# Making Q ahead of attention in seven Strassen products, and one pass of attention over K and V

## The chip, the cores and the metric

The kernel runs on one core of one Trainium2 chip. A core has five engines with instruction queues of their own: TensorE (PE, matmuls and transposes, its weight loads shown apart as PEld), VectorE (DVE), ScalarE (ACT), GpSimd (POOL) and SyncE (SP), from whose queue nearly all transfers are issued here. The time is the device time of an execution in microseconds, as the median of several runs. All arithmetic is float32. A product of two float32 matrices is made of three float32r matmuls: each operand is split into a high part (the value copied to float32r) and a low part (the difference), and high x low, low x high and high x high are added up in PSUM.

## The reference

One transformer block: layer norms modulated by a condition vector, attention against a cached K and V, and a gated FFN.

```python
def _A_ref(x, k_cache, v_cache, wq, wo):          # x (1, 2048, 576), caches (1, 16, 2048, 128)
    Hq, Dh = 32, 128
    W = min(4096, max(256, Sk // 4))              # 512: the last 512 keys
    q = (x @ wq).reshape(B, Sq, Hq, Dh).transpose(0, 2, 1, 3)
    k = jnp.repeat(k_cache[:, :, Sk - W:, :], 2, axis=1)      # 16 K/V heads, 32 query heads
    v = jnp.repeat(v_cache[:, :, Sk - W:, :], 2, axis=1)
    scores = jnp.einsum("bhqd,bhkd->bhqk", q, k) * (Dh ** -0.5)
    o = jnp.einsum("bhqk,bhkd->bhqd", _softmax(scores), v)
    return o.transpose(0, 2, 1, 3).reshape(B, Sq, Hq * Dh) @ wo

def _B_ref(x, w_gate, w_up, w_down):              # F = 4608
    return (_sigmoid(x @ w_gate) * (x @ w_up)) @ w_down

sa, ca, ga, sb, cb, gb = split(_silu(c) @ w_mod, 6)
h = _layernorm(x) * (1 + ca) + sa
x = x + ga * _A_ref(h, ...)
h = _layernorm(x) * (1 + cb) + sb
return x + gb * _B_ref(h, ...)
```

## The kernel before, in words

The 2048 tokens are four blocks of 512. The program has three stages: attention with the Q projection inside it, the output projection (`wo`), and the FFN. The last two are already made of seven Strassen products in place of eight block products; the operand sums that these need on the weight side are made during attention as background work, and parked in DRAM (`wosc`, `wsc`, `dsc`).

Attention runs over a list `seq` of 128 pairs of a head and a block: first all 32 heads for blocks 0 and 1 (half 0), then all 32 heads for blocks 2 and 3 (half 1). K and V of a group of two heads are therefore loaded and prepared twice (`load_k`, `make_k`, `load_v`, `make_v`, over `range(2 * HKV)`). Wq's columns of a head are also loaded and split once per half (`load_q`, `split_q`, `split_q_lo`).

A pair has four steps, one for each tile of 128 queries, and the main loop counts 512 of them. In step n TensorE is given a quarter of the Q projection of the pair two ahead (`qproj`, 14 matmuls a pair: four chunks of 128 channels with three each, and two for the last 64 channels, stacked twice into 128 rows), the three score matmuls of step n+2 (`scores`), four transposes of the probabilities of step n (`transp`), and three matmuls with V for the pair before (`pv`). VectorE takes each row's negative maximum from the scores (`neg`), ScalarE the exponential (`pp`) and the sum. After the transposes ScalarE copies them to float32r (the high part of `ptt`) and VectorE makes the low part. When a pair is through, the reciprocals of its sums go to DRAM (`put_rs`, tile `rscr`) and come back spread over the partitions (`get_rs`, tile `rb`), and VectorE multiplies the result of `pv` with them (`ov`); `put_o` writes it to DRAM (`oscr`).

Background work is laid out by a planner: each job gets one or two rooms (the tiles of x that are not in use), a start step, and further steps for its sums on GpSimd, its splits on ScalarE and GpSimd and its stores. There are 36 `ab` jobs (gate and up weights of 128 columns), 9 `tail` jobs (their last 32 rows) and 34 wide jobs (`wo` and `down`). A step's jobs are given out ahead of its attention work (`at_n`), or behind it (`at_late`). From step 8 on most instructions may be moved by the scheduler; those that pass `pin` or `keep_order` keep their program order, all DMAs among them.

All four blocks' normalised rows are turned into channel-major operands (`hT`), 20 transposes a block: block 0 at the start, block 1 in the first steps, blocks 2 and 3 in the middle, before half 1.

Of the kernel before, what the change touches and what calls it, by code (L numbers as in the profile page):

```python
# [9 lines left out]
F32 = mybir.dt.float32  # L10
# [6 lines left out]
P = 128  # L17
# [27 lines left out]
def adaln_block_kernel(ctx: ExitStack, tc: tile.TileContext, x, k_cache, v_cache, wq, wo, w_gate, w_up, w_down,  # L45
# [25 lines left out]
    wctx, actx = ExitStack(), ExitStack()  # L71
    wp = wctx.enter_context(tc.tile_pool(name="wp", bufs=1))
    ps = actx.enter_context(tc.tile_pool(name="ps", bufs=1, space=bass.MemoryType.PSUM))
    psw = actx.enter_context(tc.tile_pool(name="psw", bufs=1, space=bass.MemoryType.PSUM))

    def psum(tag, bufs, shape):
        return (psw if tag == "wo" else ps).tile(shape, F32, tag=tag, name=tag, bufs=bufs)

    def ps_sc():
        return psum("st", 4, [P, BLK])  # L80

    def ps_pt():
        return psum("st", 4, [P, BLK])

    def ps_qp():
        return psum("qp", 1, [P, BLK])

    def ps_ot():
        return psum("ot", 2, [P, BLK])

    def ps_wide():
        return psum("wo", 1, [P, BLK])

    def ps_wo():
        return ps_wide()[:, :D2]

    def raw_tile(shape):
        return wp.tile(shape, F32, tag="raw", name="raw", bufs=4)
# [3 lines left out]

    ident = const.tile([P, P], F32, name="ident")

# [10 lines left out]


# [8 lines left out]
    busy = raw_tile([P, P])  # L125
    nc.vector.memset(busy, 0.0)
    idle = ps_sc()
# [4 lines left out]
    tc.nc.gpsimd.memset(ones, 1.0)  # L132
    cexp = const.tile([P, NC + 1], F32, name="cexp")

# [7 lines left out]
    def mod_load(m):  # L142
        ws = []
        for j in range(2):
            w = wp.tile([P, NC, D2], F32, tag="wa", name="wm", bufs=4)
# [16 lines left out]
    def mod_half(row, j, add, loaded):  # L162
        p = ps_wo()
# [3 lines left out]

    xs = []

    for b in range(NB):  # L170
        xs.append(const.tile([P, TPB, D], F32, tag=f"x{b}", name=f"x{b}"))
# [5 lines left out]
    def bg_view(b, off, shape):  # L177
# [3 lines left out]
        v = xs[b].rearrange("p t d -> p (t d)")[:, off : off + n]  # L181
# [6 lines left out]
    LN = {}  # L188
# [41 lines left out]
    def load_a(w, n0):  # L230
        raw = raw_tile([P, NC + 1, P])
        keep_order(nc.sync.dma_start(raw[:, :NC, :], w[: NC * P, n0 : n0 + P].rearrange("(k p) n -> p k n", p=P)))
        for s in range(2):
            keep_order(nc.sync.dma_start(raw[s * TAIL : (s + 1) * TAIL, NC, :], w[NC * P :, n0 : n0 + P]))
        return raw

    def split_a_hi(raw):
        sp = wp.tile([P, 2 * NC + 1, P], F32R, tag="wa", name="wa", bufs=4)
        pin(nc.scalar.activation(sp[:, : NC + 1, :], raw, AF.Copy))
        return sp  # L240

    def split_a_lo(raw, sp):
        pin(nc.gpsimd.tensor_sub(sp[:, NC + 1 :, :], raw[:, :NC, :], f32(sp[:, :NC, :])))
        pin(nc.gpsimd.tensor_sub(sp[TAIL:, NC, :], raw[TAIL:, NC, :], f32(sp[TAIL:, NC, :])))

    def pairs_a(sp, hT):
        main, tail = hT
        out_ = []
        for k in range(NC):
            out_.append((sp[:, k, :], main[:, NC + k, :]))  # L250
            out_.append((sp[:, NC + 1 + k, :], main[:, k, :]))
            out_.append((sp[:, k, :], main[:, k, :]))
        out_.append((sp[:, NC, :], tail[:, 1, :]))
        out_.append((sp[:, NC, :], tail[:, 0, :]))
        return out_

    def load_b(w, n0):
        raw = raw_tile([P, D])
        keep_order(nc.sync.dma_start(raw, w[n0 : n0 + P, :]))
        return raw  # L260

    def split_b_hi(raw):
        sp = wp.tile([P, 2, D], F32R, tag="wb", name="wb", bufs=2)
        pin(nc.scalar.activation(sp[:, 0, :], raw, AF.Copy))
        return sp

    def split_b_lo(raw, sp):
        pin(nc.gpsimd.tensor_sub(sp[:, 1, :], raw, f32(sp[:, 0, :])))

# [8 lines left out]
    def down_mm(lhs_hi, lhs_lo, wb, j, p):  # L278
        cols = slice(j * D2, (j + 1) * D2)
        mm_seq(p, three(lhs_hi, lhs_lo, wb[:, 0, cols], wb[:, 1, cols]))  # L280
        return p


    hTs = {}
    at = actx.enter_context(tc.tile_pool(name="at", bufs=1, side="right"))

    def new_hT(b):
        main = wp.tile([P, 2 * NC, BLK], F32R, tag="hTm", name="hTm", bufs=2)
        tail = wp.tile([P, 2, BLK], F32R, tag="hTt", name="hTt", bufs=2)
        hTs[b] = (main, tail)  # L290

    sbc = at.tile([P, NC + 1, P], F32, tag="qt", name="sbc", bufs=2)
    extra = at.tile([P, 4 * P], F32, tag="rb", name="extra", bufs=2)
    scale, shift = mod_rows("scale"), mod_rows("shift")
    WM, EARLY, HN, NMR = {}, {}, {}, {}

    def load_mod(m, ks):
        if m not in WM:  # L300
            WM[m] = at.tile([P, NC + 1, D], F32, tag="ptt", name="wm0", bufs=2)
# [1292 lines left out]
```

## Time and profile before

| | |
|---|---|
| median of 3 runs | 3028.03 us (3025.97 to 3028.44) |
| the profiled execution | 3026.5 us from its first to its last instruction, which is its span |
| granted TensorE clock | 0.999 of full speed |
| first Q projection matmul | 22.89 us |
| first score row maximum, last one | 29.43 us, 1412.95 us |
| first matmul of the output projection | 1419.79 us |
| busy: PE, PEld, DVE, ACT, POOL | 3006.8, 2592.7, 2088.4, 1695.8, 1666.3 us |

Every instruction is recorded by one helper, so all have the line L36, and a group is told by its tiles: `qp<-hTm,wa` is the Q projection (`hTm`, `hTt` the channels, `wa` the split weights), `st<-kt,qt` scores, `st<-ident,pp` transposes of probabilities, `ot<-ptt,vs` the product with V, `qt<-qp` the split of Q; `x<-x` on GpSimd and ScalarE is background work, because x's tiles are its rooms. `sw<-sr,sw` is the low part of an FFN weight operand. A matmul's duration in the profile overlaps with that of the next, so the sum of durations is more than the time that passes; starts are to be compared. In a row of the grouped view stand the count, the busy time and the mean duration in ns, and the idle time of the engine before these instructions with what ended it.

### The profile page before, as it was taken

To read this page: it belongs to the slowest core of one execution; us is meant where nothing else is said; L and a number is where in the kernel's file an instruction comes from. 1 tells how busy PE (TensorE), PEld (TensorE's weight loads), DVE (VectorE), ACT (ScalarE), POOL (GpSimd) and SP (SyncE) were. 2 spreads that over 40 slices of the span, in tenths; PEclk is the share of its full clock that TensorE was granted. 3 is DMA by queue.
4 is the path that set the end of the run, shared out by engine and by line. 5 is a ranking of instruction groups with operands and counts; after the bars stand their busy time and mean duration, and the time that the engine had idled before them with its cause. 6 is when DMAs were issued, how large, how long until landed. Compare 5 with 4: busy or idle time off the path is not lost.

```text
span 3026.5 us, 49171 instructions
## 1 busy us (share of the span) xinstructions
PE 3006.8 (99%) x16644; PEld 2592.7 (86%) x16644; DVE 2088.4 (69%) x3685; ACT 1695.8 (56%) x3424; POOL 1666.3 (55%) x1558
## 2 busy tenths in 40 slices
PE   8999999999999999999999999999999999999999
PEld 7888888888888888888999988888888888888888
DVE  6666666677666666667888867666666876666667
ACT  5666666657666676555444654444444544444443
POOL 2334457634577887412555127766655566655565
PEclk9999999999999999999999999999999999999999
DMA  4677777776777777775547656555555565555554
GB/s 127 189 197 217 196 224 227 227 210 183 207 233 236 240 248 247 211 215 177 193 159 306 224 189 192 155 155 166 168 148 144 161 204 140 143 148 142 144 138 119
DMA packets 485788, 571.32 MB, mean 189 GB/s; under 512 B 52000, under 2 KB 434208, under 8 KB 476832
## 3 DMA queue, kind: packets, MB, share of 16 engines
q1 hardware_dynamic: 484400, 567.65, 63.1%
q8 instruction: 132, 2.16, 0.3%
q14 instruction: 120, 0.98, 0.1%
q10 hardware_dynamic: 1136, 0.53, 0.1%
HBM read 394.33 MB, written 173.70 MB: 188 GB/s over the span
## 4 chain that ended last, share of the span: by engine, by line
PE 94%; DVE 2%; issue 1%; POOL 1%; DMA 1%; ACT 1%; SPq 0%; POOLq 0%; DVEq 0%; ACTq 0%
PE a L36 21%; PE st L36 18%; PE w L36 13%; PE qp L36 13%; PE ot L36 11%; PE c L36 11%; PE b L36 5%; DVE x L36 1%; POOL x L36 1%; PE wo L36 1%; SPq L36 0%; DVE ptt L36 0%; ACT pp L36 0%; DVE neg L36 0%; DVE hc L36 0%
## 5 line engine op out<-in xcount | busy, mean ns | idle before, releaser
L36 DVE TENSOR_TENSOR x<-w,x 128x288 f32<-128x288 f32 x964 | 421.4, 452 | 249.4 <-PE w L36 246.8
L36 PE MATMUL a<-hc,sw 128*128 128x512 f32 x2016 | 583.4, 395 | 1.4 <-DVE v L36 1.3
L36 DVE TENSOR_REDUCE neg<-st 128x1 f32<-128x512 f32 x512 | 352.4, 688 | 275.6 <-PE st L36 274.9
L36 ACT ACTIVATE ptt<-st 128x512 fp32r<-128x512 f32 x512 | 306.0, 598 | 391.0 <-PE st L36 390.0
L36 PE MATMUL ot<-ptt,vs 128*128 128x512 f32 x1536 | 483.5, 423 | 1.8 <-DVE ptt L36 1.7
L36 PE MATMUL st<-kt,qt 128*128 128x512 f32 x1536 | 443.4, 395 | 0.4 <-ACT pp L36 0.4
L36 PE MATMUL qp<-hTm,wa 128*128 128x512 f32 x1524 | 440.5, 398 | 2.3 <-DVE hTm L36 1.2
L36 DVE TENSOR_TENSOR ptt<-st,ptt 128x512 fp32r<-128x512 f32 x512 | 351.9, 688 | 126.6 <-ACT ptt L36 126.3
L36 PEld LDWEIGHTS a<-hc,sw 128*128 128x128 f32 x2016 | 356.4, 188 | 41.6 <-DVE v L36 2.8
L36 ACT ACTIVATE pp<-st,neg 128x512 f32<-128x512 f32 x512 | 350.4, 684 | 43.7 <-DVE neg L36 42.6
L36 ACT ACTIVATE sw<-sr 128x384 fp32r<-128x384 f32 x504 | 257.9, 519 | 189.1 <-issue 90.0
L36 POOL TENSOR_TENSOR sw<-sr,sw 128x256 fp32r<-128x256 f32 x245 | 200.4, 819 | 282.8 <-ACT sw L36 282.6
L36 PEld LDWEIGHTS st<-kt,qt 128*128 128x128 f32 x1536 | 286.7, 188 | 66.9 <-ACT pp L36 1.1
L36 PEld LDWEIGHTS w<-wh,hl 128*128 128x128 f32 x1776 | 297.2, 188 | 51.2 <-DVE x L36 2.7
L36 PEld LDWEIGHTS qp<-hTm,wa 128*128 128x128 f32 x1524 | 281.5, 188 | 69.5 <-DVE qt L36 7.1
L36 PE MATMUL w<-wh,hl 128*128 128x288 f32 x1776 | 327.5, 296 | 0.4 <-DVE x L36 0.3
L36 POOL TENSOR_TENSOR x<-x 128x256 f32<-128x256 f32 (+3 forms) x342 | 254.4, 763 | 117.8 <-DMA x<-in_B_w_up_dram 58.6
L36 PEld LDWEIGHTS st<-ident,pp 128*128 128x128 f32 x2048 | 254.3, 140 | 70.4 <-ACT pp L36 0.8
L36 PE MATMUL st<-ident,pp 128*128 128x128 f32 x2048 | 307.0, 273 | 0.5 <-DVE ptt L36 0.3
L36 PE MATMUL c<-hc,sw 128*128 128x512 f32 x1008 | 302.9, 394 | 0.0
L36 DVE TENSOR_TENSOR sw<-sr,sw 128x256 fp32r<-128x256 f32 x259 | 189.9, 733 | 141.0 <-ACT sw L36 113.2
L36 PEld LDWEIGHTS ot<-ptt,vs 128*128 128x128 f32 x1536 | 252.9, 190 | 30.7 <-DVE ptt L36 4.2
(239 smaller groups left out, 5043.6 us busy)
## 6 DMA issues: line engine op xcount, KB each, us to landing
sr<-wsc SPq DMA_DIRECT2D x504, 192.0 KB
wh<-dsc SPq DMA_DIRECT2D x144, 288.0 KB
dsc<-x SPq DMA_DIRECT2D x34, 1008.0 KB
vr<-oscr SPq DMA_DIRECT2D x32, 1024.0 KB
rb<-rscr SPq DMA_DIRECT2D x126, 256.0 KB
wsc<-x SPq DMA_DIRECT2D x36, 896.0 KB
oscr<-ov SPq DMA_DIRECT2D x63, 512.0 KB
wosc<-x SPq DMA_DIRECT2D x32, 1008.0 KB
```

The source lines that it names most:

```text
L36: i = got(*args, **kw)
```

## The change

All of Q is made before attention begins. The 576 channels are two halves of 288, the 2048 tokens two pairs of blocks, and two heads that share K and V are taken together: a 2x2 block product, which takes seven products on sums of operands instead of eight. Each of the 32 units u (16 pairs of heads, for blocks 0 and 1 and then for blocks 2 and 3) has seven products of seven matmuls with 512 columns: twice three for 128 channels, and one for the last 32, whose three combinations are stacked into one operand of 128 rows. Weight sums are made by GpSimd (`w_sums`), weight operands split by ScalarE (high) and VectorE (low, two instructions: `w_split`). The channel sums T1 to T4 are made on the chip. Results are scaled, go to `qo` tiles, and are stored to DRAM (`qscr`) by SP. This takes 224 steps of one product each ahead of step 0. In the first 16 only block 0 is needed, and its products are kept in room tiles (`first_room`). Blocks 2 and 3 are normalised and turned in some 50 of the steps, 24 transposes a block.

Attention then runs over 16 groups with all four blocks of both heads in each, so K and V are loaded and prepared once. Q of a pair is loaded 13 steps ahead and split 6 steps ahead by ScalarE and GpSimd (`load_qt`, `split_qt`). In a step TensorE gets the scores of step n+2, the V product five steps behind, and the transposes, which have two PSUM banks of their own (`pt`). Background jobs are given out from step -200 on, in eight rooms instead of four, with other distances. All instructions up to the end of attention keep their program order.

On TensorE a step in the middle of attention was, with a piece of the Q projection on both sides:

```order
L36 MATMUL qp<-hTm,wa 128x512 x2
L36 MATMUL qp<-hTt,wa 128x512 x2
L36 MATMUL st<-kt,qt 128x512 x3
L36 MATMUL st<-ident,pp 128x128 x4
L36 MATMUL ot<-ptt,vs 128x512 x3
L36 MATMUL qp<-hTm,wa 128x512 x3
```

and now is, where K of the next group is transposed too:

```order
L36 MATMUL st<-kt,qt 128x512 x3
L36 MATMUL ot<-ptt,vs 128x512 x3
L36 MATMUL pt<-ident,pp 128x128 x4
L36 MATMUL st<-ident,kv 128x128 x4
L36 MATMUL st<-kt,qt 128x512 x3
```

The projection has left the step, and the V product stands ahead of the transposes.

On VectorE, in the first 16 products (`sw<-raw,sw` is the low part of a weight operand in two instructions, `qo<-b` a result's eviction, the others are block 1's channel operands and sums):

```order
L36 TENSOR_TENSOR x_111<-hs,x_111 128x512 x2
L36 TENSOR_TENSOR sw<-raw_77,sw 128x256
L36 TENSOR_TENSOR sw<-raw_77,sw 32x128
L36 SCALAR_TENSOR_TENSOR qc<-st,scol,qc 128x512 x2
L36 TENSOR_TENSOR qc<-x_111,qc 128x512 x2
L36 TENSOR_TENSOR x_111<-shift,x_111 128x512
L36 TENSOR_TENSOR sw<-raw_77,sw 128x256
L36 TENSOR_TENSOR sw<-raw_77,sw 32x128
L36 SCALAR_TENSOR_TENSOR qo<-b,x_114 128x512
```

These are new; the weight operands of the next products stand between them.

On SP, in the stretch of wide jobs, from before (`dsc`, `wosc` a wide job's stores, `in_B_w_down` its loads):

```order
L36 DMA rscr_284<-rs 128x4
L36 DMA x_101<-in_B_w_down_dram 128x288 x4
L36 DMA rb<-rscr_284 128x512
L36 DMA sscr_293<-sx 512x1x128
L36 DMA dsc_342<-x_104 128x2016
L36 DMA dsc_342<-x_103 128x2016
L36 DMA rscr_281<-rs 128x4
L36 DMA raw<-in_A_k_cache_dram 128x512
L36 DMA rb<-rscr_281 128x512
```

and of the change:

```order
L36 DMA rscr_335<-rs 128x4
L36 DMA qr<-qscr_3_134 128x512
L36 DMA rb<-rscr_335 128x512
L36 DMA wosc_408<-x_113 128x7x288
L36 DMA wosc_408<-x_112 128x7x288
L36 DMA xr_4663<-in_A_wo_dram 128x288 x4
L36 DMA rscr_336<-rs 128x4
L36 DMA qr<-qscr_3_134 128x512
L36 DMA rb<-rscr_336 128x512
```

Between the store of a pair's reciprocals and their load now stands the load of a Q.

The diff, cut to its core:

```diff
+    def load_raw(u):
+        raw, n0 = RAW[u % 2], u % HKV * 2 * P
+        t = raw.rearrange("p s (h n) d -> p s h (n d)", h=2)
+        for h in range(2):
+            nc.sync.dma_start(t[:, 0:2, h], wqh[: 2 * P, h, n0 : n0 + 2 * P].rearrange("(s p) n -> p s n", p=P))
+        for r in range(3):
+            nc.sync.dma_start(t[r * TQ : (r + 1) * TQ, 2], wqh[2 * P :, :, n0 : n0 + 2 * P])
...
+    def w_split(u, a, src=None):
...
+        t = SWQ[u, a] = sw_tile([P, 5, P])
+        nc.scalar.activation(t[:, 0:3, :], src, AF.Copy)
+        nc.vector.tensor_sub(t[:, 3:5, :], src[:, 0:2], f32(t[:, 0:2, :]))
+        nc.vector.tensor_sub(t[2 * TQ : 3 * TQ, 2, :], src[2 * TQ : 3 * TQ, 2], f32(t[2 * TQ : 3 * TQ, 2, :]))
...
+    def q_product(u, a, c, p, fresh):
+        w, h = SWQ.pop((u, a)), QC[c]
+        pairs = []
+        for s in range(2):
+            pairs.append((w[:, s, :], h[:, s, :]))
+            pairs.append((w[:, 3 + s, :], h[:, s, :]))
+            pairs.append((w[:, s, :], h[:, 3 + s, :]))
+        pairs.append((w[:, 2, :], h[:, 2, :]))
+        for n, (l, r) in enumerate(pairs):
+            nc.tensor.matmul(p, l, r, start=fresh and n == 0, stop=n == len(pairs) - 1, skip_group_check=not fresh)
...
+    def q_store():
+        u, i = stores.pop(0)
+        nc.sync.dma_start(qscr[u // HKV][u % HKV][:, i], QOUT.pop((u, i)))
...
+        else:
+            n -= 2
+            at_n(n - (8 if u == EARLY else 10), load_raw, u)
+            at_n(n - 5, w_sums, u, (S1, S2))
+            at_n(n - 4, w_sums, u, (S4, S3))
+            for a, d in ((A11, 3), (S1, 1), (A12, 0), (S2, -1), (A22, -2), (S4, -2), (S3, -3)):
+                at_n(n - d, w_split, u, a)
...
+    for g in range(HKV):
+        for half in range(2):
+            seq += [(half, 2 * g + i, 2 * half + b) for i in range(2) for b in range(2)]
...
+    def split_qt(b):
+        raw = QR.pop(b)
+        t = QT[b] = at.tile([P, 2, BLK], F32R, tag="qt", name="qt", bufs=2)
+        keep_order(nc.scalar.activation(t[:, 0, :], raw, AF.Copy))
+        nc.gpsimd.tensor_sub(t[:, 1, :], raw, f32(t[:, 0, :]))
...
+    for b in range(NBLK):
+        at_n(TPB * b - 13, load_qt, b)
+        at_n(TPB * b - (6 if b > 1 else 5 - b), split_qt, b)
...
-    free = {0: 9, 1: 9, 2: 7, 3: 7}
-    n, due = 9, 9.0
+    SPANS = {r: [(NLO + 24, SW0 - 22), (ROOMS_FREE, N - 42)] if r < 2 else [(ROOMS_FREE, N - 42)] for r in range(NB)}
+    for r in range(NB, NB + XR):
+        SPANS[r] = [(2, N - 42)]
+    HOLD = {"ab": 14, "tail": 22, "wo": 22, "down": 22}
...
-            at_n(n + 4 + part, bg_sums, k, part)
+            at_n(n + 6 + (part if kind == "ab" else 2 * part), bg_sums, k, part)
             if kind != "ab":
-                at_n(n + 6 + 2 * part, bg_split, k, part)
+                at_n(n + 10 + 3 * part, bg_split, k, part)
...
-        due = max(due, n - 2) + {"ab": 4.6, "tail": 7.6}.get(kind, 5.9)
+        due = max(due, n - 2) + {"ab": 6.0, "tail": 10.0}.get(kind, 8.5)
...
-        b, i = divmod(n, TPB)
-        bq, part = divmod(n - 1, TPB)
-        if bq + 2 == 3:
-            if n > 6:
-                qproj(3, 2 * (n - 7))
-                qproj(3, 2 * (n - 7) + 1)
-        elif ok(bq + 2):
-            qproj(bq + 2, part)
+        b, i = divmod(n - 5, TPB)
+        if n < 0:
+            q_step(*order[n - NLO])
+            waiting += [n] * (len(stores) - len(waiting))
         if 0 <= n + 2 < N:
             scores(n + 2)
+        if ok(b):
+            pv(b, i)
         if 0 <= n < N:
             transp(n)
         if 0 <= n + 2 < N:
             expo(n + 2)
-        if ok(b - 1):
-            pv(b - 1, i)
```

More of the change, by code (lines that the diff above doesn't have):

```diff
@@ L884, in adaln_block_kernel, with fits @@
+    free = {r: SPANS[r][0][0] for r in SPANS}
+    n = NLO + 24
+    due = float(n)
     while jobs or wide:
         assert n < N - 44, (n, len(jobs), len(wide))
-        got = [r for _, r in sorted((free[r], r) for r in range(NB) if free[r] <= n)
-               if not (r > 1 and n1 - 55 < n < n1 + 4)]
-        two = n > 130 and len(got) > 1 and wide and (not jobs or not n1 - 55 < n < n1 + 4)
-        if due > n or not got or not (two or jobs):
+        def fits(kind):
+            return [r for _, r in sorted((free[r], r) for r in SPANS if free[r] <= n and
+                                         any(lo <= n and n + HOLD[kind] <= hi for lo, hi in SPANS[r]))]
+        k, rooms = None, ()
+        if wide and n > 40 and len(fits("wo")) > 1 and (wide[0][0] == "wo" or n > 92):
+            k, rooms = wide.pop(0), fits("wo")[:2]
+        elif jobs and fits(jobs[0][0]):
+            rooms = fits(jobs[0][0])[:1]
+            k = jobs.pop(0)
+        if due > n or k is None:
+            if k is not None:
+                (jobs if k[0] in ("ab", "tail") else wide).insert(0, k)
```

766 lines of the change are left out of this document (463 added, 303 removed).

## Prediction

> **What bounds the kernel now.** I read the page's busy times first.
>
> ```profile
> span 3026.5 us, 49171 instructions
> ...
> PE 3006.8 (99%) x16644; PEld 2592.7 (86%) x16644; DVE 2088.4 (69%) x3685; ACT 1695.8 (56%) x3424; POOL 1666.3 (55%) x1558
> ```
>
> TensorE is busy for nearly the whole span and nothing else comes near it, so time is won by taking work from TensorE, as long as no other queue then falls behind. A matmul's duration overlaps with the next, so its price is read from starts in the timeline. These are the last attention steps, where the last Q projection has just ended and no other follows:
>
> ```profile
> 1400.13 0.62 PE L36 MATMUL qp<-hTt,wa 128*128 128x512 f32 x2
> 1400.60 0.85 PE L36 MATMUL st<-kt,qt 128*128 128x512 f32 x3
> 1401.28 0.60 PE L36 MATMUL st<-ident,pp 128*128 128x128 f32 x4
> 1401.64 0.94 PE L36 MATMUL ot<-ptt,vs 128*128 128x512 f32 x3
> ...
> 1406.12 0.86 PE L36 MATMUL st<-kt,qt 128*128 128x512 f32 x3
> ```
>
> Two Q matmuls take 0.47 us of TensorE, so one costs 0.235; four transposes take 0.36, so one costs 0.09. From 1400.60 to 1406.12 lie three steps without any Q work: 1.84 us each. The reductions (x144 in VectorE's column, one a step), counted over a long stretch, give the step with Q:
>
> ```profile
> 817.00:1202.00 385.00, 99.28 (x144) 111.35 (x288) 1.00 0.77 242
> ```
>
> 385/144 = 2.67 us (the last two columns are DMA share and GB/s). 1.84 + 3.5 Q matmuls x 0.235 = 2.66: this stretch runs at TensorE's own pace, with all the background work in it. The Trainium skill ("TensorE: Matmul & The Clock Gate", Back-to-back issue gap) gives some 131 ns for a sustained matmul of 512 columns; the trace shows 235 for these float32r ones, and by the page the first term below would be -29 us instead of -53. The measurement decides.
>
> **The change, part by part.** *TensorE.* The grouped view has all of the old projection, but for its second block (14 matmuls in another bank):
>
> ```profile
> L36 PE MATMUL qp<-hTm,wa 128*128 128x512 f32 x1524 | 440.5, 398 | 2.3 <-DVE hTm L36 1.2 <-DVE qt L36 0.7
> L36 PE MATMUL qp<-hTt,wa 128*128 128x512 f32 x254 | 79.8, 396 | 0.0
> ```
>
> 1524 + 254 + 14 = 1792 matmuls become 32 x 7 x 7 = 1568: 224 x 0.235 = -53 us. K is transposed 16 times instead of 32: -64 x 0.09 = -6. The blocks' transposes grow from 80 to 96: +1.
>
> I make the sum as a new timeline up to the first output-projection matmul, since all behind it is the same code:
>
> ```profile
> 22.89 3.06 PE L36 MATMUL qp<-hTm,wa 128*128 128x512 f32 x12 [1.17 <-DVE hTm L36]
> ...
> 1419.79 1.78 PE L36 MATMUL a<-wh,vh 128*128 128x288 f32 x12
> ```
>
> The start reaches its first projection through the same steps as now, with four more transposes: 23.5. Then 1568 x 0.235 = 368; transposes of blocks 1 to 3, 72 x 0.09 = 6; 512 steps x 1.84 = 942; K, 64 x 0.09 = 6; filling and draining the deeper pipeline (PV now runs five steps behind), 3 by estimate. That is 1349, against 1419.8 now: -71 us if no step waits. (53 + 6 - 1 is 58 of it. The other 13 are waits of the old attention: it takes 1396.9 us from 22.89 on, and these prices give 512 x 2.66 + 20 for K's and the blocks' transposes and the tail, 1383.)
>
> *What the other engines must do in 1.84 us.* Their price is also a spacing:
>
> ```profile
> 251.27 0.60 ACT L36 ACTIVATE ptt<-st 128x512 fp32r<-128x512 f32 x1 [0.98 <-PE st L36]
> ...
> 251.76 0.68 ACT L36 ACTIVATE pp<-st,neg 128x512 f32<-128x512 f32 x1
> ...
> 252.34 0.20 ACT L36 ACTIVATION_READ_ACCUMULATOR pp<-st,neg 128x1 f32 x1
> ...
> 255.03 1.06 DVE L36 TENSOR_TENSOR ov<-ot,rb 128x512 f32<-128x512 f32 x1
> ...
> 256.05 0.69 DVE L36 SCALAR_TENSOR_TENSOR qt<-qp,qt 128x512 fp32r<-128x512 f32 x1
> ...
> 256.66 0.68 DVE L36 TENSOR_REDUCE neg<-st 128x1 f32<-128x512 f32 x1
> ...
> 257.26 0.68 DVE L36 TENSOR_TENSOR ptt<-st,ptt 128x512 fp32r<-128x512 f32 x1
> ```
>
> ScalarE per step: 0.49 + 0.58 + about 0.1 = 1.17; the split of the loaded Q, 0.5 every fourth step, 0.13; the two splits of a wide weight job (below: 1.16 + 0.92 every 8.5 steps) 0.24: 1.54, or 84%. VectorE: 0.60 + 0.60 + a quarter of 1.02 = 1.46, 79%; the Q part leaves it. GpSimd:
>
> ```profile
> L36 POOL TENSOR_TENSOR x<-x 128x288 f32<-128x288 f32 x144 | 113.4, 808 | 4.9
> L36 POOL TENSOR_TENSOR x<-x,gate 128x576 f32<-128x576 f32 x68 | 95.7, 1429 | 9.6 <-DMA x<-in_A_wo_dram 8.8
> L36 POOL TENSOR_TENSOR x<-x,x 128x1152 fp32r<-128x1152 f32 x35 | 93.7, 2676 | 33.7 <-ACT x L36 29.4 <-DMA sscr<-sx 2.7 <-DMA raw<-in_A_v_cache_dram 0.6
> L36 POOL TENSOR_TENSOR x<-x,x 128x864 fp32r<-128x864 f32 x33 | 67.8, 2056 | 48.2 <-ACT x L36 38.6 <-DMA raw<-in_A_wq_dram 2.7 <-PE st L36 2.7
> L36 ACT ACTIVATE x<-x 128x1152 fp32r<-128x1152 f32 x35 | 40.7, 1164 | 1.8 <-POOL x L36 1.8
> L36 ACT ACTIVATE x<-x 128x864 fp32r<-128x864 f32 x33 | 30.4, 921 | 0.0
> L36 POOL TENSOR_TENSOR vs<-raw,vs 128x512 fp32r<-128x512 f32 x32 | 41.5, 1297 | 140.8 <-ACT vs L36 126.7 <-DMA rscr<-rs 11.2 <-issue 2.9
> ```
>
> A wide job is 370 us / 34 = 10.9, every 8.5 steps: 1.28 a step; Q's low part, a form like the last row's 1.30, every fourth: 0.33; V, 0.04: 1.65, or 90%. So nobody exceeds TensorE, but nobody has much left. Behind a wide job's split on ScalarE, which waits for GpSimd's sums, stand the copy and exponential of the step. An exponential is due on TensorE two steps later; by the spacings above it is ready 1.6 us early, which covers one 1.16 us split but not one that also waits. Loss in attention: at least nothing (the 1.84 us steps), at most what DMA can cost (first rival); I take 22 us, some 2%, twice the 1% lost now.
>
> *DMA.* SP gains 128 stores and 128 loads of Q (256 KB each) and loses half of K and V and little of Wq. The sizes:
>
> ```profile
> rb<-rscr SPq DMA_DIRECT2D x126, 256.0 KB
> ...
> oscr<-ov SPq DMA_DIRECT2D x63, 512.0 KB
> wosc<-x SPq DMA_DIRECT2D x32, 1008.0 KB
> ...
> 259.28 0.57 SPq L36 DMA_DIRECT2D wsc<-x  x1
> ```
>
> In a wide stretch 6.5 old steps (17.4 us) carry one job of 2.6 MB (two such stores and 0.6 MB of loads), and 8.5 new ones (15.6 us) do: 150 GB/s become 167. A block of four steps carries reciprocals 256 KB, outputs 256, Wq 160, K and V 128 in 10.7 us; now 256, 256, Q 256 and 64 in 7.4 us: 75 GB/s become 112. The share goes from 0.77 to 0.77 x 279/225 = 0.95. The trace has 0.85 without any loss of pace (43 us, 16 steps), nothing higher for long:
>
> ```profile
> 1288.00:1331.00 43.00, 43.00 (x223) 35.32 (x222) 27.88 (x44) 25.96 (x58) 8.13 (x10) 1.00 0.85 246
> ```
>
> A tail job's 24 stores, 0.57 each on SP, stand in four steps: 13.7 us, where four steps are now 7.4. The reciprocals' load and the next Q load queue up behind them some 6 us late; a multiplication of VectorE waits for the former, and behind that the low part of the step's transposed probabilities. Five of the nine tail jobs lie in the attention; a few us each are in the 22.
>
> *The Q phase.* Each product is 7 x 0.235 = 1.64 us of TensorE. VectorE makes the low part of every weight operand, in two instructions. The nearest row is the FFN's:
>
> ```profile
> L36 DVE TENSOR_TENSOR sw<-sr,sw x259: 405/426/1568, 1746.6 to 2998.4; 128x256 fp32r<-128x256 f32 x130
> ...
> 1882.36 1.29 POOL L36 TENSOR_TENSOR hl<-v,hl 128x512 fp32r<-128x512 f32 x1
> ...
> 1882.64 1.29 DVE L36 TENSOR_TENSOR sw<-sr,sw 128x256 fp32r<-128x256 f32 x1 [1.11 <-DMA scr<-h]
> ```
>
> It takes 0.43, and up to 1.57 when it meets GpSimd: here it ends 0.28 behind GpSimd's. With 0.25 for the 32x128 part (between nothing and 0.43: half the columns pull it down, a fixed part of each instruction up) and 0.60 for an eviction (2 of 7 products; all of them in the first eight pairs), VectorE has 0.85 a step, 1.28 early. In the first 16 steps it also normalises block 1 and makes its sums. Block 0's rows give the former: four of the first, four scalings, and 13 small steps of 0.2, 10 us.
>
> ```profile
> 4.08 0.82 DVE L36 BATCH_NORM_STATS2 st<-x 128x6 f32<-128x288 f32 x2 [2.97 <-DMA x<-in_A_x_dram]
> ...
> 14.73 3.04 DVE L36 TENSOR_TENSOR h<-h,scale 128x576 f32<-128x576 f32 x4 [2.58 <-ACT h L36]
> ```
>
> With some 15 passes of 0.69, 13 weight splits and 10 evictions that is 35 us, while TensorE has 28. I take +12 there (0 to 25) and +11 for the rest: meetings with GpSimd, and the stretch in which blocks 2 and 3 are made (0 to 30).
>
> The sum: -71 + 12 + 11 + 22 = -26 from a span of 3026.5: 3000.5. The runs' median, 3028.03, stands 1.5 above the span: **3002 us**.
>
> **Rivals.** (1) *DMA and its queue become the bound in the wide stretch (steps 46 to 335), slower.* SP issues in order, and each block's reciprocals go out and come back through DRAM; SP stands until they have landed.
>
> ```profile
> SPq L36 <- DMA rscr<-rs: 224.8, 83, 6.0
> ...
> 902.41 0.33 SPq L36 DMA_DIRECT2D rscr<-rs  x1
> ...
> 905.65 0.33 SPq L36 DMA_DIRECT2D rb<-rscr  x1
> ```
>
> If the engines then drain for 1.5 of these 3.2 us, a block needs 0.95 x 7.4 + 1.5 = 8.5 us, 2.13 a step: 290 x 0.29 = +84, less the 22 counted: 3064. It decides once a wide step passes 1.84 + (26 + 22)/290 = 2.0. Against it: 0.85 did no harm, and Q is loaded seven steps ahead. (2) *VectorE and GpSimd hold the Q phase.* GpSimd has four 128x384 sums per pair (about 1.0 each, between the 0.81 and the 1.30 of its rows) and four of 0.7 every six steps for gate and up: 1.0 a step, early 1.2. If VectorE waits out all of it, a step has 0.85 + 1.0 = 1.85 instead of 1.64, over 168 steps +35, and early 1.28 + 1.2 = 2.5, over 56 steps +48: 83 instead of 23, 3062. At 0.6 of it the time is 3029, no change. For it speaks the 1.57 row; against it that GpSimd is not always there. The Trainium skill ("SBUF — State Buffer", Who interferes with whom) states it as a rule: a VectorE instruction with two SBUF inputs and a GpSimd one that reads SBUF exclude each other for the whole instruction. By that rule, with which the 1.29 us row agrees, the attention is free of it, since its VectorE operations read PSUM, and the Q phase is not. (3) *Nearly all arrives*: losses of only 25: 2980. (4) *The products are not fewer*: excluded, the new TensorE order has 1568.
>
> **How the numbers follow.** Forecast (2990 to 3017) 0.46; nearly all 0.22; Q phase held 0.14; DMA 0.16; 0.02 for what I don't see. About 0.2% (6 us) is what a measurement of this kernel can tell. Faster: 0.46 + 0.22 + a fifth of the Q case = 0.71; same: half of the Q case and a little of the DMA one, 0.09; slower 0.20. The range leaves out the lower tail below 2970 and the worse half of both slow cases: 2970 to 3052; without the cases of the other sign it would be 2975 to 3020.
>
> **What would show it.** Right: TensorE records down by some 270, a Q phase of 224 products in 380 to 400 us, attention steps of 1.84 to 1.9 us, the first output projection near 1394. Wrong: reductions more than 2.0 us apart at a DMA share over 0.9 (first rival); products more than 1.8 us apart with VectorE waiting beside GpSimd (second); or a loss behind the attention, where I expect none.

## The result and the profile after

The changed kernel takes 3250.44 us (median of 4 runs, 3245.03 to 3254.14) against 3027.86 for the kernel before: 1.0734 times as long, 95% interval 1.0719 to 1.0749. The forecast was 3002. Differences of less than some 8 us between two versions of the changed kernel are not read as effects below, since its own runs spread by 9.

The page of the changed kernel, busy times and the chain that ended last:

```profile
span 3252.3 us, 50928 instructions
...
PE 3023.0 (93%) x16375; PEld 2579.5 (79%) x16375; DVE 2323.0 (71%) x4113; ACT 1814.1 (56%) x3727; POOL 1846.8 (57%) x1680
...
PE 58%; DMA 10%; issue 4%; DVE 3%; POOL 3%; SPq 2%; ACT 2%; DVEq 0%; POOLq 0%; ACTq 0%
PE a L36 19%; PE w L36 12%; PE c L36 10%; PE st L36 5%; PE b L36 5%; PE ot L36 5%; DMA rb<-rscr 4%; DMA rscr<-rs 4%; PE pt L36 3%; SPq L36 2%; DVE ptt L36 1%; POOL x L36 1%; DVE neg L36 1%; ACT pp L36 1%; POOL qt L36 1%
```

TensorE has 269 records fewer, as the change says, and is no longer always busy. Before, TensorE had 94% of the chain; now it has 58%, and the way of the reciprocals through DRAM (`rscr<-rs`, `rb<-rscr`) has 8% of the whole span, though it exists in a third of it only.

Where the time went, by stretch. TensorE's Q products, and the row maxima of attention (x512, in VectorE's column), each from the first to the last; the last two columns are DMA share and GB/s, the one before them the granted clock:

```profile
22.90:492.00 469.10, 391.09 (x1568) 0.95 0.65 198
```

```profile
490.00:1640.50 1150.50, 346.96 (x512) 397.23 (x1022) 0.95 0.78 228
```

```profile
1647.28 1.76 PE L36 MATMUL a<-wh,vh 128*128 128x288 f32 x12
```

The Q phase takes 469 us, where the forecast had 397 (368 + 6 + 12 + 11); attention takes 2.25 us a step, 1150, where it had 970 (942 + 6 + 22). The output projection's first matmuls come at 1647 instead of 1394. Behind them 1605 us pass, and 1607 passed before: nothing changed there. So the miss of 250 us is 180 in attention and 72 in the Q phase.

**Attention.** The view of waits, from 490 to 1645 us (total, times, longest):

```profile
DVE ov L36 <- DMA rb<-rscr: 131.9, 47, 7.8
...
PE pt L36 <- DVE ptt L36: 125.4, 51, 8.1
```

and the same view for SyncE's queue:

```profile
SPq L36 <- DMA rscr<-rs: 261.0, 94, 5.9
SPq L36 <- POOL qt L36: 104.5, 65, 4.5
```

VectorE stands for the reciprocals 47 times, and TensorE stands for VectorE about as often and as long. In the kernel before no wait for `rb` appears among VectorE's. One such place in the timeline, of SyncE's queue, VectorE and TensorE:

```profile
962.42 0.38 SPq L36 DMA_DIRECT2D rscr<-rs  x1
965.24 0.32 SPq L36 DMA_DIRECT2D qr<-qscr  x1
965.61 3.37 SPq L36 DMA_DIRECT2D sscr<-sx  x2
969.03 0.67 SPq L36 DMA_DIRECT2D oscr<-ov  x1
969.79 0.60 SPq L36 DMA_DIRECT2D rb<-rscr  x1
...
975.41 1.07 DVE L36 TENSOR_TENSOR ov<-ot,rb 128x512 f32<-128x512 f32 x1 [3.30 <-DMA rb<-rscr]
976.39 0.69 DVE L36 TENSOR_TENSOR ptt<-pt,ptt 128x512 fp32r<-128x512 f32 x1
976.99 0.68 DVE L36 TENSOR_REDUCE neg<-st 128x1 f32<-128x512 f32 x1
...
977.22 0.63 PE L36 MATMUL pt<-ident,pp 128*128 128x128 f32 x4 [2.46 <-DVE ptt L36]
```

The sums are stored at 962.42; their load is issued 7.4 us later, behind a Q load, two stores of output sums and one of outputs, and has landed after another 5.6. VectorE has stood 3.3 us by then, and the low part of a step's probabilities and the next row maximum stand behind its multiplication. That closes a loop: the late row maximum delays the sums of the block after next.

**The Q phase**, in five stretches: the first 28 products in two pieces, products 28 to 100 (with the 48 transposes of blocks 2 and 3 near its end), 100 to 126 (VectorE makes sums and low parts of the channel operands of blocks 2 and 3), and the rest. The columns are busy times of PE, PEld, DVE, ACT and POOL:

```profile
22.90:73.80 50.90, 33.74 (x136) 24.98 (x137) 42.15 (x87) 29.92 (x56) 13.89 (x13) 0.90 0.33 98
73.80:104.60 30.80, 23.22 (x92) 16.89 (x91) 27.70 (x46) 11.23 (x23) 19.49 (x18) 0.94 0.43 131
104.60:246.20 141.60, 127.75 (x553) 101.35 (x552) 115.78 (x223) 63.50 (x122) 73.93 (x83) 0.96 0.70 215
246.20:310.30 64.10, 47.60 (x183) 35.30 (x183) 57.83 (x82) 31.76 (x65) 38.25 (x32) 0.95 0.39 123
310.30:492.00 181.70, 164.67 (x694) 131.97 (x694) 132.57 (x221) 85.30 (x175) 103.40 (x114) 0.96 0.83 249
```

At the forecast's 1.64 us a product these are 26, 20, 118, 43 and 161 us of matmuls. In the first, second and fourth VectorE is busy for 83 to 90% of the time and TensorE for 66 to 75%. In the other two TensorE is busy for 90%; they lose 23 and 21 us, in part in single stalls, of which this is one, on SyncE's queue and VectorE:

```profile
426.26 7.50 SPq L36 DMA_DIRECT2D wsc<-x  x13
433.86 1.71 SPq L36 DMA_DIRECT2D qscr<-qo  x2
...
438.74 0.69 DVE L36 SCALAR_TENSOR_TENSOR qo<-c,gate 128x512 f32<-128x512 f32 x1 [7.11 <-DMA qscr<-qo]
```

Thirteen stores of a tail job stand ahead of a store of Q; its buffer is not free, VectorE cannot write the next result out, and TensorE's next product finds no bank.

### The profile page after: what moved, and what is told of

It is laid out like the page before. It is cut to its first block, busy times and chain, and to the rows that moved or that the text cites. A ratio compares the mean times of both kernels' runs of the same rounds, so it can differ in the third digit from the quotient of the medians.

```text
span 3252.3 us, 50928 instructions
## 1 busy us (share of the span) xinstructions
PE 3023.0 (93%) x16375; PEld 2579.5 (79%) x16375; DVE 2323.0 (71%) x4113; ACT 1814.1 (56%) x3727; POOL 1846.8 (57%) x1680
## 4 chain that ended last, share of the span: by engine, by line
PE 58%; DMA 10%; issue 4%; DVE 3%; POOL 3%; SPq 2%; ACT 2%; DVEq 0%; POOLq 0%; ACTq 0%
PE a L36 19%; PE w L36 12%; PE c L36 10%; PE st L36 5%; PE b L36 5%; PE ot L36 5%; DMA rb<-rscr 4%; DMA rscr<-rs 4%; PE pt L36 3%; SPq L36 2%; DVE ptt L36 1%; POOL x L36 1%; DVE neg L36 1%; ACT pp L36 1%; POOL qt L36 1%
## 5 line engine op out<-in xcount | busy, mean ns | idle before, releaser
L36 PE MATMUL st<-kt,qt 128*128 128x512 f32 x1536 | 504.6, 438 | 1.1 <-POOL qt L36 1.1
L36 DVE TENSOR_TENSOR ptt<-pt,ptt 128x512 fp32r<-128x512 f32 x512 | 351.6, 687 | 152.9 <-ACT ptt L36 152.1
L36 PE MATMUL ot<-ptt,vs 128*128 128x512 f32 x1536 | 453.3, 404 | 4.8 <-DVE ptt L36 4.3
L36 PE MATMUL pt<-ident,pp 128*128 128x128 f32 x2048 | 323.3, 282 | 130.1 <-DVE ptt L36 125.4
L36 PEld LDWEIGHTS pt<-ident,pp 128*128 128x128 f32 x2048 | 260.2, 145 | 220.9 <-issue 126.4
L36 POOL TENSOR_TENSOR qt<-qr,qt 128x512 fp32r<-128x512 f32 x128 | 165.5, 1293 | 371.7 <-ACT qt L36 354.1
L36 ACT ACTIVATE ptt<-pt 128x512 fp32r<-128x512 f32 x512 | 304.8, 595 | 115.4 <-PE pt L36 113.2
L36 PEld LDWEIGHTS ot<-ptt,vs 128*128 128x128 f32 x1536 | 296.4, 194 | 82.3 <-DVE ptt L36 12.9
L36 PE MATMUL a<-qc,sw 128*128 128x512 f32 (+1 forms) x912 | 238.4, 407 | 46.1 <-DVE qo L36 28.3
L36 POOL TENSOR_TENSOR hl<-vs,hl 128x512 fp32r<-128x512 f32 x139 | 192.0, 1382 | 107.7 <-ACT hl L36 104.3
```

The source lines that it names most:

```text
L36: i = got(*args, **kw)
```

## The experiments

Times are medians; "Q" and "attention" are read in the profiled execution, "Q" is the time from the first to the last Q product, "attention" from the first to the last row maximum.

| run | time | Q | attention |
|---|---|---|---|
| changed kernel | 3250.4 | 469 | 1150 |
| a1_no_trip | 3118.7 | 474 | 1008 |
| a2_later | 3187.5 | 470 | 1078 |
| a3_no_ws | 3219.8 | 447 | 1140 |
| a4_late_q | 3257.3 | 472 | 1153 |
| b1_tails | 3223.7 | 463 | 1123 |
| b2_later3 | 3166.1 | 470 | 1057 |
| b3_no_low | 3193.1 | 422 | 1134 |
| b4_both | 3152.2 | 467 | 1051 |
| c1_actq | 3292.6 | 494 | 1162 |
| c2_mod | 3250.9 | 467 | 1150 |
| c3_all | 3227.2 | 491 | 1097 |
| c4_sum | 3142.0 | 449 | 1056 |
| d1_merge | 3220.6 | 462 | 1120 |
| d2_best | 3136.6 | 457 | 1040 |
| d3_sum | 3043.1 | 410 | 995 |
| e1_old_merge, e2_old_spread | 3027.4, 3028.1 | | |

**The way through DRAM left out.**

```diff
             if b < NBLK - 2:
-                at_late(n - 1, put_rs, b)
-                at_late(n + 1, get_rs, b)
+                RB[b] = ONE_RB[0]
...
```

> The changed kernel, without the way of the reciprocals of the row sums through DRAM: none is stored or loaded, and VectorE multiplies the V product with a constant tile of ones (so the output is not normalised, the last two pairs apart). Theory A (the attention of the changed kernel, 1150 us from the first row maximum to the last, is held by a loop: sums, store, stand of SyncE until it has landed, load, multiplication, and behind it on VectorE the next row maxima): the attention falls to 950-1000 us, 1.87-1.95 a step, and the whole time by 150-200, to 3050-3100. Theory B (the 16 DMA engines' throughput holds it, share 0.81 in the middle): the loads were 0.25 of some 2.2 MB a block, so at most a ninth goes: attention 1030-1100, time 3140-3200. Theory C (GpSimd or ScalarE hold it): attention 1120-1150.

Attention fell by 143 us to 1008, the whole by 132: nearer A than B, and between their ranges. The middle of that run steps at 299.6/161 = 1.86 us, close to the 1.84 of the prediction, and its engines are about as busy there as the prediction counted: VectorE 83%, ScalarE 87%, GpSimd 92%, where it had 79, 84 and 90 (the first line has PE, PEld, DVE, ACT and POOL, the second the row maxima in VectorE's column).

```profile
742.90:1042.50 299.60, 297.09 (x1620) 243.70 (x1619) 249.35 (x407) 260.06 (x569) 274.63 (x212) 1.00 0.74 250
```

```profile
742.90:1042.50 299.60, 108.78 (x161) 124.32 (x320) 1.00 0.74 250
```

The run leaves out the transfers together with the wait for them, so it does not tell throughput from lateness by itself; the next two runs do.

**The same transfers, but more time for them.** The multiplication comes three steps later in b2_later3 (two in a2_later), and the sums and the store of the outputs move back with it; the diff is of the former:

```diff
-            nc.vector.tensor_mul(OT[unit][:, :, blk % 2, :], ...)
+            if b < NBLK - 3:
+                at_late(TPB * b + TPB - 1 + 5 + 3, norm, b)
...
-                at_late(n + 1, get_rs, b)
+                at_late(n + 2, get_rs, b)
```

> The changed kernel, with the multiplication of a pair's V product by the reciprocals given out two steps later (stores of the outputs one step later, sums of outputs two). Same work, same transfers. Theory A: two more steps, some 3.7-4.4 us, are given to the round trip, whose lateness was 2.8 us on average where VectorE waited for it (132 us in 47 waits); attention 1000-1060 us, time 3100-3160. Theory B (throughput) and C (GpSimd, ScalarE): no change, attention 1140-1160, time 3240-3260.

> The changed kernel with the multiplication by the reciprocals three steps later and the load of the reciprocals one step later. Theory A, all of it: the loop now has three more steps than the change gave it, and SyncE should hardly stand for the store to land (261 us before): attention 1010-1050 us where it is 1008 without any reciprocals, time 3110-3150. If the 70 us between the run with two steps more (1078) and that without reciprocals (1008) are the transfers themselves and not lateness: attention 1065-1085, time 3170-3190.

Two steps gave 63 us of the whole time; three steps and the later load gave 84, and 93 of attention. Theories B and C had forecast no change for the first of these runs. VectorE's waits for the reciprocals went from 131.9 us to

```profile
DVE ov L36 <- DMA rb<-rscr: 13.5, 11, 3.1
```

so lateness is shown as the larger part of the loop's price. Throughput was not the bound: b2_later3 has every transfer, and its steps 192 to 288, in the stretch of wide jobs, take 188.4/96 = 1.96 us at a DMA share of 0.89, where the middle of the changed kernel took 568/258 = 2.20 at 0.81 (row maxima again in VectorE's column; b2_later3 first).

```profile
910.00:1098.40 188.40, 65.38 (x96) 74.65 (x192) 1.00 0.89 281
```

```profile
612.00:1180.00 568.00, 174.96 (x258) 200.04 (x515) 0.97 0.81 243
```

Both runs ended somewhat above theory A's range: 50 us between b2_later3 and the run without reciprocals are not lateness of this load, but what the round trip takes of SyncE and the DMA engines, or lateness of other things behind it; these two were not told apart.

The lead in numbers, from the end of a block's reciprocal on VectorE to the start of its multiplication, as a mean over the 126 blocks that go through DRAM: 16.8 us in the kernel before, where VectorE stood 0.5 us in all for it; 14.3 in the changed kernel, with 152 us of standing ahead of these multiplications; 20.1 in b2_later3. In the 47 blocks of the changed kernel whose multiplication waited for the load, VectorE was ready 12.5 us after the reciprocal on average, and the load let it start after 15.3. The old lead of 16.8 us is 6.3 steps of 2.67; at 1.84 that is 11.6, or 13.4 with the one step by which the change puts the V product further back.

**SyncE's stand for the Q buffer.**

```diff
-        at_n(TPB * b - 13, load_qt, b)
+        at_n(TPB * b - 11, load_qt, b)
```

> The changed kernel with the load of a pair's Q given out 11 steps ahead instead of 13, three steps behind GpSimd's split of the pair before the last, whose buffer it takes, instead of one. SyncE stood 104 us for that split in the attention. If this stand is part of theory A's loop: it falls below 40 us, and the time by 20-60, to 3190-3230. If it only takes up time that SyncE would have stood for the reciprocals anyway: 3240-3260.

No gain (3257.3). SyncE's stand for the buffer fell from 104.5 us to 8.6, and its stand for the reciprocals' store to land rose from 261 to 381: the stand for Q only took up time that SyncE would have stood anyway, the second branch of the expectation.

**VectorE and GpSimd in the Q phase.**

```diff
     def raw_of(u, a):
-        return RAW[u % 2][:, :, {A11: 0, A21: 1, A12: 2, A22: 3}[a], :]
+        return RAW[u % 2][:, :, {A11: 0, A21: 1, A12: 2, A22: 3, S1: 1, S2: 3, S4: 2, S3: 0}[a], :]
 
     def w_sums(u, which):
+        return
```

> The changed kernel without GpSimd's weight sums in the Q phase: the products that take sums are given the plain quarters of Wq instead (so Q is wrong), split by ScalarE and VectorE as before. Theory D (VectorE's low parts stand while GpSimd works, 448 instructions of 0.57 us mean where they take 0.35 undisturbed): the low parts fall from 256 us to 170-185, the Q phase from 462 us (24 to 487) to 390-415, time 3180-3205. Theory E (the Q phase is held by the loads of Wq, the stores of Q and the two stretches in which VectorE normalises blocks): phase 440-460, time 3230-3250.

```diff
-        nc.vector.tensor_sub(t[:, 3:5, :], src[:, 0:2], f32(t[:, 0:2, :]))
-        nc.vector.tensor_sub(t[2 * TQ : 3 * TQ, 2, :], ...)
...
-            pairs.append((w[:, 3 + s, :], h[:, s, :]))
+            pairs.append((w[:, s, :], h[:, s, :]))
```

> The changed kernel without VectorE's low parts of the Q phase's weight operands (448 instructions, 256 us); the matmuls that took them take the high parts again, so Q lacks that term, with as many matmuls. Theory G (VectorE, in program order, holds the Q phase, by its own work more than by meetings with GpSimd, of which taking away GpSimd's sums gave only 22 of 469 us back): Q phase 385-410 us, time 3165-3195. Theory E (SyncE's queue and the loads hold it): 440-460 us, time 3220-3245.

The low parts of the changed kernel, by tile:

```profile
L36 DVE TENSOR_TENSOR sw<-ws,sw x256: 282/425/1506, 73.5 to 484.2; 128x256 fp32r<-128x256 f32 x128
L36 DVE TENSOR_TENSOR sw<-raw,sw x192: 283/425/1496, 20.6 to 482.6; 128x256 fp32r<-128x256 f32 x96, 32x128 fp32r<-32x128 f32 x96
```

They take 256 us, 0.57 each. The half of them that no GpSimd instruction overlaps take 0.28 us (small) and 0.42 (large), the other half 0.80 on average; all at the former would be 157 us. The Trainium skill ("SBUF — State Buffer", Who interferes with whom) has such instructions exclude GpSimd's reads of SBUF, and this spread to 1.5 us agrees. Without GpSimd's weight sums they fell to 192 us, yet the Q phase by only 22: theory D's range was missed. 94 of the 448 still met GpSimd's other work there, so this prices the meetings with the weight sums alone. Without any low parts the Q phase fell by 47 us, to 422, which is outside theory G's 385 to 410; that the time lies in G's range is due to 16 us in attention, of which the theory says nothing. So theory G is right on the mechanism and too high in size. In that run VectorE has 131 us of work left in 422, and what still stalls TensorE is the store of Q behind tail stores, and block 1's work in the first 16 products (44 us for 26 of matmuls).

**The tail jobs' stores.**

```diff
...
-        for part in range(4 if kind == "tail" else 1):
-            at_n(n + (9 if kind == "ab" else 16 if kind == "tail" else 16) + part, bg_store, k, part)
+        for part in range(8 if kind == "tail" else 1):
+            at_n(n + (9 if kind == "ab" else 16) + part, bg_store, k, part)
```

> The changed kernel, with the 24 stores of a tail job given out as three in each of eight steps instead of six in each of four. Same stores, same bytes. Theory F (SyncE's queue: a tail's stores take 13.7 us of it in four steps, and what is queued behind, Wq's loads in the Q phase, reciprocals and Q in attention, comes late): the stretches of products 72 to 88 and 188 to 204, 35.5 and 36.8 us for 26.3 us of matmuls, lose most of their excess, five more tails lie in the attention; time 3190-3225. If the stores are slow because of the many short rows that the DMA engines move, wherever they are issued: no change, 3240-3260.

> The tail jobs of three stores a step and the multiplication three steps later together, the whole computation. Theories A and F: the sum of the two gains, since they lie on the same queue perhaps 10 to 20 us less: 3070-3120. If one of them stands in for the other: no better than the better of the two.

27 us less, at the edge of F's range, and most of it in attention; the two stretches of the Q phase, which were to lose most of an excess of 9.2 and 10.5 us, fell by 2.2 and 3.7 only. Together with the later multiplication 3152.2, outside the range expected for both: short of the sum of the two gains (111) by 13.

```diff
-                    pin(nc.sync.dma_start(wsc[f + q][to * TQ : (to + 1) * TQ, a:b, 2, :], src[rows]))
+                    pin(nc.scalar.dma_start(wsc[f + q][to * TQ : (to + 1) * TQ, a:b, 2, :], src[rows]))
```

> The changed kernel with the tail jobs' stores issued from ScalarE's queue instead of SyncE's; their places in the program, their bytes and their rows stay. Theory F (SyncE's time for issuing: in a run of 13 tail stores, 7.5 us, a store of Q waits, its buffer is not free, VectorE cannot write the next result out, TensorE waits): the stretches of products 72 to 88, 156 to 172 and 188 to 204 (35.5, 30.0, 36.8 us) come to 27-30 each, the attention loses 15-40 us, time 3185-3215. If the stores' many short rows hold the DMA engines, or ScalarE pays as much as SyncE is given: 3235-3265.

42 us slower, outside both ranges. Two of the three stretches that were named came down (30.0 to 27.5 and 36.8 to 29.4 us), but the first rose from 35.5 to 42.6 and attention by 12. The stalls went to ScalarE, which now stands until its queue has issued the stores (waits of that run from 23 to 1680 us):

```profile
ACT ptt L36 <- DMA wsc<-x: 39.3, 9, 9.3
ACT ptt L36 <- DMA wsc<-xr: 27.4, 6, 6.8
ACT qo L36 <- PE a L36: 23.8, 17, 6.8
ACT gate L36 <- DMA wsc<-x: 18.9, 4, 5.7
ACT sw L36 <- DMA wsc<-x: 17.8, 4, 6.5
```

An issue costs on either queue. Fewer of them help:

```diff
-            raw = bg_view(rooms[0], 0, [4, P])
-            BG[k] = raw, bg_view(rooms[0], 4 * P, [4, P]), ...
+            raw = bg_view(rooms[0], 0, [8, P])
+            BG[k] = raw, raw[:, 4:8], ...
...
-        return [(0, 3, r[:, 0:3, :]), (3, 7, m)]
+        return [(0, 7, r[:, 1:8, :])]
```

> The changed kernel with a tail job's planes laid next to each other, so that its 24 stores become 16 with the same bytes and rows. Theory F (number of issues, on whichever queue): 8 x 0.56 = 4.5 us less of SyncE for each of nine jobs; the excess of products 72 to 88 and 188 to 204 (9.2 and 10.5 us) falls by a third or more, time 3215-3238. If bytes and rows count: 3244-3256.

30 us less with the same bytes, in theory F's range (the two runs of it lie 10 us apart); in the profiled executions the Q phase lost 7 us and attention 30. The two stretches fell by 0.8 and 3.0 us, less than the third that F had, so the gain is not where the theory put it. Nor is it the number of issues alone: as many stores, given out further apart, gained nearly as much (b1_tails). The same edit in the kernel before:

> The kernel before, with 16 stores in a tail job instead of 24, the same bytes. Its stretches of 16 steps with a tail job took 2.72 to 2.80 us a step where others took 2.67, 1 to 2 us for each of nine jobs. If the issues are the price there too: 3017-3024. If the old kernel's longer steps hide them (13.7 us of SyncE against 10.7 us of steps, with reserves of the reciprocals behind): 3025-3029, no change.

> The kernel before, with 16 stores in a tail job, given out over five steps instead of four. As the run beside it, and 1 to 3 us less again if SyncE's queue is the price: 3014-3023; otherwise 3025-3029.

Ratios to the kernel before 1.000 (0.999 to 1.0009) and 1.000 (0.9991 to 1.0009): nothing, against the first branch of both expectations. With steps of 2.67 us the 24 stores are hidden; with the changed kernel's shorter ones they are not.

**Another lead counted in steps.**

```diff
-            at_n(n + 3 + c, lambda m, c: mod_sum(wm[m], c), m, c)
+            at_n(n + 7 + c, lambda m, c: mod_sum(wm[m], c), m, c)
...
-            at_n(n + 9 + j, mod_make2, key, m, j, add)
+            at_n(n + 13 + j, mod_make2, key, m, j, add)
```

> The changed kernel with the sums and matmuls of the four modulation vectors four steps later, seven and thirteen steps behind their load instead of three and nine. Theory H (every lead of the old kernel is counted in steps, and a step is shorter now; this one was 3 x 2.67 us and is 3 x 1.84): ScalarE's stands for these loads (20.6 us) go, and with them the stalls of TensorE near steps 13, 37, 61 and 85: 15 to 35 us, time 3213-3235. Otherwise 3244-3256.

ScalarE's stands for these loads fell from 20.6 us to 3.3 and the time did not change, so this lead was not one that mattered; theory H does not hold for every lead.

**Several at once.** No new edits. c3_all and c4_sum have the tail stores on ScalarE's queue and came out 97 and 117 us above their ranges; c3_all differs from b2_later3 by these stores and the later modulation vectors alone, and is 61 us slower. d2_best and d3_sum have 16 stores on SyncE's queue, two a step; d2_best lies in the range expected.

> The multiplication three steps later, its load one step later, the tail stores from ScalarE's queue and the modulation vectors four steps later, together; the whole computation. If the three causes stand side by side: 3250 less 84 less 35 less 25, 3105; by range 3080-3130. It does not reach the kernel before (3028), since VectorE's work in the Q phase and the block operands are not touched.

> All named causes taken away at once, to see whether they make up the difference: the reciprocals' way through DRAM left out (the V product is multiplied with ones), the low parts of the Q phase's weight operands left out, the tail stores on ScalarE's queue, the modulation vectors later. The output is therefore not the reference's. If the causes are these: 3250 - 132 - 57 - 35 - 25 = 3001, range 2980-3025, which is where the forecast was. If something large is still unnamed: 3040 or more.

> The whole computation with the multiplication three steps later, the load of the reciprocals one step later, 16 stores in a tail job and two of them a step. With 24 stores, three a step, it was 3152. Theory F: 3125-3145. Otherwise 3146-3158.

> All causes taken away as far as possible, with ScalarE left out of it: no way of the reciprocals through DRAM (the V product is multiplied with ones), no low parts of the Q phase's weight operands (the matmuls take the high parts), 16 stores in a tail job, two a step; so the output is not the reference's. If the causes add up: 3250 - 132 - 57 - 35 = 3026, range 3005-3042, still above the forecast by what block 1 to 3's operands cost VectorE. If they stand in for each other, or one is still unnamed: 3050 or more.

The Q products and the attention of d3_sum, in the views shown above:

```profile
22.80:432.70 409.90, 374.00 (x1568) 0.98 0.74 227
```

```profile
430.80:1425.50 994.70, 347.33 (x512) 397.09 (x1022) 0.99 0.71 230
```

3043.1, 1 us beyond the range for "the causes add up" and 41 above the forecast: 207 of the 248 us of the miss go with these three edits, two of which leave out work and not only its lateness. The single gains (132, 57, and 30 for the tail stores, which is d2_best beside b2_later3) sum to 219, so they overlap by some 12. The rest is Q, 410 us for 374 of matmuls and transposes, and attention's first 96 steps, 2.0 to 2.35 us a step in pieces of 16; no run took these apart. The best whole computation is d2_best, 3136.6: 1.0359 times the kernel before (1.0329 to 1.0389). No version found is faster than the kernel before.

## Why the prediction was wrong, step by step

- **TensorE's floor was right, and a product's price 3% too high.** 269 records fewer, and 1.83 to 1.9 us an attention step without the round trip. Products 56 to 72 took 26.3 us, the 16 x 1.64 of the forecast, but with small waits in them; without, in b3_no_low and d3_sum, they took 25.4, 1.59 each. That makes the Q matmuls 356 us in place of 368, and the losses below, which are counted from 368, 12 us larger. The output projection and FFN did not change.
- **"I take 22 us" for attention was the step that failed; the loss was 200.** The prediction compared each engine's busy time with 1.84 us and found room, and it named the late reciprocals only for the five tail jobs, "a few us each". Every lead in the program is counted in steps, and the steps became a third shorter while SyncE got a load per block more. A lead of 16.8 us would have become 13.4, and in the blocks whose multiplication waited the way took 15.3. It was a latency, not a busy time, so no sum of busy times showed it; the busy times themselves were counted about right, as the middle of a1_no_trip shows.
- **The first rival named the right place and a wrong price and condition.** It had SyncE's stand for the sums, but as a drain of 1.5 us a block at a DMA share of 0.95, 84 us; the steps came to 2.25 us at a share of 0.78 (2.20 at 0.81 in the middle), and throughput was not the bound, as the 1.96 us steps of b2_later3 at a share of 0.89 show. The share itself was well sized: 0.95 at 1.84 us comes to 0.89 at 1.96.
- **The Q phase's losses, +12 and +11, were undersized by 72 us.** The first 16 products took 51 us, where the term had VectorE at 35 us of work and 12 of loss on TensorE's 28: 23 of loss, within the 0 to 25 that it allowed. It is the +11 for the rest (0 to 30) that failed: of the 95 lost above matmuls and transposes it had the other 72. The low parts cost 256 us of VectorE, 1.14 a product, where the step of 0.85 had 0.68 for them. The stretch with the channel operands of blocks 2 and 3 took 64 us for 43. And the stores of Q behind a tail job's were not in the sum: the four tails in that stretch were put at nothing.
- **The second rival (VectorE and GpSimd, 3062) had nearly the size of the Q phase's loss, 83 us against 95 above its matmuls,** but not its whole mechanism: taking away the weight sums gave 22 us, taking away the low parts themselves 47. That the sizes are close is in part luck. Its no-change point, 3029, is 0.6 of the 83 us; if VectorE waited out 0.6 of GpSimd's time, the prediction's own prices give only the early 56 steps a loss, 20 us, which the 23 already covered.
- **The other rivals** (nearly all arrives; products not fewer) are ruled out.

The chance of 0.20 for slower came from two rivals taken one at a time. Both came at once, and a third of the same kind (issues) beside them, while the range took each as the exception. Even the two at their full price, 62 and 60 us, would have made 3124.

## What to carry to other kernels

When a change makes a loop's step shorter, every distance counted in steps becomes shorter in time: list each store, load and wait whose lead is in steps, multiply by the new step, and compare with the latency that the trace shows from the first instruction to the use, waits on the issuing queue included. Busy shares below 100% on every engine say nothing of such a loop. Work that was free in a slow loop, such as 24 issues of 0.56 us, has a price in a fast one, and the price depends on how many stand together on a queue: here fewer issues, or the same ones further apart, took some 30 us less, and the same ones on ScalarE's queue 42 us more.

## What the runs showed of the hardware

The granted clock falls when TensorE stands. Two views of the changed kernel, a piece of TensorE's timeline and windows of 3 us (columns as in the Q phase's stretches):

```profile
65.42 3.15 PE L36 MATMUL b<-qc,sw 128*128 128x512 f32 x7 [8.91 <-DVE qo L36]
68.41 1.78 PE L36 MATMUL a<-qc,sw 128*128 128x512 f32 x7
```

```profile
60.00:63.00 3.00, 0.00 (x0) 0.00 (x0) 3.00 (x3) 0.28 (x1) 3.00 (x3) 0.73 0.00 0
63.00:66.00 3.00, 0.58 (x2) 0.51 (x3) 2.90 (x5) 0.00 (x0) 0.96 (x1) 0.50 0.16 45
66.00:69.00 3.00, 3.00 (x10) 2.38 (x9) 2.27 (x6) 2.85 (x6) 0.00 (x0) 0.63 0.12 42
69.00:72.00 3.00, 1.19 (x6) 0.63 (x4) 2.97 (x4) 1.01 (x3) 2.63 (x2) 1.00 0.58 192
```

After a stand of 8.91 us TensorE starts again at half clock: the seven matmuls of the next product take 2.99 us from their start to that of the one behind, where 1.59 is the time without waits, and from 69 us on the clock is back at 1.00. The Trainium skill ("TensorE: Matmul & The Clock Gate", Part 1: The HAM clock gate) describes this: half rate after an idle window of some 3.4 us, until a busy one has passed; the trace agrees. So a stall costs more than its length: the clock's mean was 0.95 in Q phase and attention of the changed kernel, 0.98 and 0.99 in d3_sum and 1.00 before. The prediction had no term for it. How much of the stalls' price is clock was not measured by itself. An upper estimate comes from TensorE's busy time with the same matmuls: 391 us for the 1568 Q matmuls against 374 in d3_sum, and 1011 against 970 in a1_no_trip from the first row maximum to some 5 us behind the last, so up to 17 us of the Q phase's loss and 42 of the 143 that went with the round trip.
